# Converting float64 weights to fp32 on chip: signs and exponents by two parametric Relus on ScalarE, mantissas joined as integers, and the last products and the last store issued another way

## The chip, the cores and the metric

The kernel runs on one core of one Trainium2 chip. The metric is the device time of one execution in microseconds, as the median of several. A core has five engines with queues of their own: TensorE (PE, with its weight loads PEld), VectorE (DVE), ScalarE (ACT), GpSimd (POOL) and SyncE (SP), which here only issues DMAs. They wait for each other by semaphores; each takes its own instructions in the order in which the program gives them.

## The reference

Two blocks are computed, the second on the result of the first. The first is a recurrence over 768 steps for 4 batches and 8 heads, with a state of 40 x 40 for each; the second is a feed-forward block with the gate h * clip(h + 3, 0, 6) / 6.

```python
# r, k, v, w, a, b: (4, 8, 768, 40), float32
for t in range(S):
    y[:, :, t] = einsum('bhd,bhde->bhe', rt, state)
    Sa = einsum('bhde,bhe->bhd', state, at)
    state = state * wt[:, :, None, :] - einsum('bhd,bhe->bhde', Sa, bt) \
            + einsum('bhd,bhe->bhde', vt, kt)
x = y.transpose(0, 2, 1, 3).reshape(3072, 320)
h = x @ w_in                                  # 320 x 2048
out = (h * clip(h + 3.0, 0.0, 6.0) / 6.0) @ w_out     # 2048 x 320
```

The two weight matrices come as float64 (a division by a float64 root made them so), everything else as float32. [...] the kernel reads the weights as pairs of 32-bit words and makes fp32 of them itself.

## The kernel before

**Units and groups.** The sequence is cut into blocks of 64 steps; a unit is one block of two batches, with all 8 heads. There are 24 units, in groups of four. For a unit the recurrence becomes matrix products: running products of w (a scan on VectorE, L484) and their reciprocals (L495, L510), scaled a, b and k (at L513, bt L521, kt L603), scores (L458, masked by L467), the inverse of a triangular matrix, and from these the update of the state (sn, L865 and L874), the output y (L889, then yg, L898 to L904) and a transposed copy of it, xt, moved by DMAs from SBUF to SBUF (L918, L923).

**The inversion.** It is done for a whole group at once (invert, from L643). F is transposed in blocks of 32 (fb, L648), masked on POOL (L651), then 30 steps follow, each a product (prod, L660) and an addition (x, L666), each dependent on the one before; two transposes (tb L669, tt L674) end it. third_block (L696 to L729) completes the 64 x 64 inverse tinv.

**The feed-forward block.** For each unit there are two jobs of half the hidden features each. expand makes 24 products (L974; the trace records each fp32 product as two), of which 8 use the third part of the 320 features, win2 (these are the "short" ones); ScalarE and VectorE make the gate of them (gt, L989 and L990) in two halves; contract makes 8 products with wout (L1015), ScalarE copies the sum out (L1033) and two DMAs store it (L1038). While spread is on, a job's short products are not issued by expand but through narrow, by contract of the job before, after its sixth product (LATEST), or by the recurrence.

**The weights.** load_weights is a generator. There are 20 pieces of 128 x 512 weights, 512 KB of raw data each. A piece's raw words lie in one of eight homes, places whose own use comes later (tinv, parts of win and wout, the inversion's tiles), with low words and high words alternating. Its loads are issued on SyncE (L277), and a home is only loaded again when the conversion that frees it is in the program (the list free). Piece 15 needs piece 8 done, 16 needs 9, 17 needs 13, 18 needs 14, 19 needs 15.

Before the change the conversion of a piece is: the exponent field, shifted down, by VectorE (L299); ScalarE subtracts 896, times 2^23, with a Relu (L301); VectorE puts the sign bit on (L320); VectorE makes 2^23 plus the high mantissa bits as a float (L325), ScalarE scales that (L328); VectorE adds the low word times 2^-52 (L307) and multiplies by the power of two (L312). L307 and L312 of a piece come after L299 of the next one, so the pieces overlap by one.

**What sets the order of the work.** The schedule is manual: the order of the Python calls is the order of each engine's instructions, and generators are advanced to mix them. In the first group, by_twos runs the preparation of four units two by two (aside runs one step of the inversion). The weights' generator is advanced by one yield: by run, when a weight (its argument fill) is given; by aside, for each step, with the weight MIXED; in the loop after it (L1133 to L1142), at every third step of the inversion; then while phase says that a conversion is in a certain state; and from the list PLAN on, which orders the four first units' own work (U, UT, sn, H, y, move), 1.5 or 3 times for each entry, with the rest of the weights after it. limit says how many loads may have been issued so far. In the same loop tinv is cleared on POOL when two pieces are converted. The feed-forward jobs start when half the pieces (for the first half of units 0 and 1) or all of them are converted and the unit's xt is there; from then on pieces() mixes the feed-forward products with the recurrence to the end, and the last lines (while jobs or next(stream)) issue what is left.

Of the kernel before, what the change touches and what calls it, by code (L numbers as in the profile page):

```python
# [16 lines left out]
P = 128  # L17
BL = 64
HB = BL // 2
L = 32  # L20
SLOT = 64


def _ap(ap, extra, dims):
# [5 lines left out]
def kernel(  # L30
# [42 lines left out]
    nc = tc.nc  # L73
# [34 lines left out]
    def ps_pair(*dims):  # L108
# [19 lines left out]
        out=ident[:], in_=ones, pattern=[[1, P]],  # L128
# [4 lines left out]
        out=ones[:, 0:BL], in_=ones[:, 0:BL], pattern=[[1, BL]],  # L133
# [3 lines left out]
        out=ones[BL:P, 0:BL], in_=ones[BL:P, BL:P], pattern=[[1, BL]],  # L137
# [6 lines left out]
    nc.vector.memset(three[:], 3.0)  # L144
    warm = const.tile([P, 1], F32, name="warm")
    nc.scalar.activation(out=warm[:], in_=three[:], func=AF.Relu)
    low = const.tile([P, 1], F32, name="low")
    nc.vector.memset(low[:], -896.0 * 2 ** 23)


    AHEAD = NU + 1
# [33 lines left out]
    for i in range(3):  # L185
        t = const.tile([P, H, BL], F32, name=f"score{i}")
# [36 lines left out]
    converted = [0]  # L223
    phase = [0]
# [30 lines left out]
    def load_weights():  # L255

        todo, homes = weight_pieces(), raw_homes()
        loaded, done, issued = deque(), [], [0]
        upcoming = []

        def load():
            if issued[0] == min(PIECES, limit[0]):
                return False
            if not upcoming:
                upcoming.append(next(homes))
            raw, before = upcoming[0]  # L270
            if before is not None and before not in done:
                return False
            upcoming.clear()
            issued[0] += 1
            out, loads = next(todo)
            for to, src in loads(raw):
                nc.sync.dma_start(out=to, in_=src)  # L277
# [12 lines left out]
        for n in range(PIECES + 1):  # L290
            now = None
            if n < PIECES:
                while load():
                    pass
                out, raw = loaded.popleft()
                hi = raw[:, :, :, 1]
                x = parts[n % 2]
                now = out, raw, x
                nc.vector.tensor_scalar(x, hi, 20, 0x7FF, ALU.logical_shift_right,  # L299
                                        ALU.bitwise_and)  # L300
                nc.scalar.activation(out=x, in_=x, func=AF.Relu, bias=low[:], scale=2.0 ** 23)  # L301
                phase[0] = 1
                yield
            if before:
                out, raw, y = before
                m, yf = raw[:, :, :, 1].bitcast(F32), y.bitcast(F32)
                nc.vector.scalar_tensor_tensor(m, raw[:, :, :, 0], 2.0 ** -52, m, ALU.mult, ALU.add)  # L307
                phase[0] = 2
                yield
                if len(out.shape) == 4:  # L310
                    m, yf = (z.rearrange("p n (j c) -> p n j c", c=out.shape[3]) for z in (m, yf))
                nc.vector.tensor_tensor(out=out, in0=m, in1=yf, op=ALU.mult)  # L312
                converted[0] += 1
                done.append(n - 1)
                while load():
                    pass
                phase[0] = 3
                yield
            if now:
                nc.vector.scalar_tensor_tensor(x, hi, 0x80000000, x, ALU.bitwise_and,  # L320
                                               ALU.bitwise_or)
                phase[0] = 4
                yield

                nc.vector.tensor_scalar(hi, hi, 0xFFFFF, 0x4B000000, ALU.bitwise_and,  # L325
                                        ALU.bitwise_or)
                m = hi.bitcast(F32)
                nc.scalar.activation(out=m, in_=m, func=AF.Copy, bias=-7.0, scale=2.0 ** -20)  # L328
                phase[0] = 5
                yield  # L330
            before = now

    def weight_pieces():

# [47 lines left out]
    NK = NG * NU  # L382
# [65 lines left out]
    def half(i, n=SLOT):  # L448
        return slice(SLOT * i, SLOT * i + n)
# [489 lines left out]
    narrow, spread, LATEST = [], [False], 2  # L939
# [67 lines left out]
    def contract(i, r, gts):  # L1007
        split = i < SPLIT
        if r == 0 or split:
            op = bank("o", [P, DM], 1)  # L1010
        else:
            op = sums.pop(i)
        for c in range(2):
            for n in range(NQ):
                nc.tensor.matmul(out=op[:], lhsT=gts[c][:, n, :],  # L1015
                                 rhs=wout[:, c * HJ + r * NQ + n, :],
                                 start=((split or r == 0) and c == 0 and n == 0),
                                 stop=((split or r == 1) and c == 1 and n == NQ - 1))
                if n % 2 and (c == 0 or n < NQ - 1):
                    yield True  # L1020
        if r == 0:
            sums[i] = op
            if split:
                part = ffn.tile([P, 3 * P], F32, name="part", tag="xt", bufs=6)[:, 0:DM]
                nc.scalar.activation(out=part, in_=op[:], func=AF.Copy, scale=1.0 / 6.0)
                sums[i] = part
        else:
            ob = ffn.tile([P, DM], F32, name="ob", bufs=OB)
            if split:
                nc.vector.scalar_tensor_tensor(out=ob[:], in0=op[:], scalar=1.0 / 6.0,  # L1030
                                               in1=sums.pop(i), op0=ALU.mult, op1=ALU.add)
            else:
                nc.scalar.activation(out=ob[:], in_=op[:], func=AF.Copy, scale=1.0 / 6.0)  # L1033
            del ready[i]
            g, p = names[i]
            for q in range(2):
                row = (2 * p + q) * T + g * BL
                nc.sync.dma_start(out=out[row:row + BL, :], in_=ob[half(q)])  # L1038
        yield True


# [45 lines left out]

    STAGES = 9

    RFETCH, EARLY, MIXED = 8, 5, 1 / 3  # L1090
    TWOS = 14

    def by_twos(first, steps, mixed, rate, fill={}):


        chains = [by_stages(first + i, prepared(first + i)) for i in range(NU)]
        for t in range(TWOS):

# [14 lines left out]
    for name in "WABK":  # L1113
        for i, engine in enumerate((nc.sync, nc.scalar if name == "W" else nc.sync)):
            fetch(name, i, engine)
    for t, _ in enumerate(by_twos(0, 4, MIXED, 0, {5: 1, 6: 1, 10: 1})):
        if t == 0:
            next(weights)
        limit[0] = {7: 4, 10: 12}.get(t, limit[0])
        while t == 7 and refill[0]():  # L1120
            pass
        if t == RFETCH:
            fetch("R", 0)
# [8 lines left out]
    n, cleared = 0, []  # L1132
    while not third:  # L1133
        aside(1)
        if not third:
            n += 1
            if n % 3 == 1:
                next(weights, None)
            if converted[0] == 2 and not cleared:
                cleared.append(nc.gpsimd.memset(tinv[:], 0.0))  # L1140
            if n % EARLY == 0 and early:
                run(early.popleft())  # L1142
    assert not early and cleared
# [161 lines left out]
    m = 0  # L1305
# [60 lines left out]
```

## Time and profile before

| | |
|---|---|
| median of three runs | 831.4 us (829.04 to 831.72) |
| the profiled execution | 831.98 us; its span, first to last instruction, 830.2 us |
| mean granted TensorE clock | 0.938 |
| busy: TensorE / weight loads | 746.4 us (90%) / 632.0 us (76%) |
| busy: VectorE / ScalarE / POOL | 547.4 us (66%) / 321.7 us (39%) / 156.1 us (19%) |
| HBM read / written | 34.08 MB / 3.93 MB |

The page gives the busy time of each engine, then the span in 40 slices of 20.8 us: a digit is the busy share of an engine in tenths, and the row PEclk gives the TensorE clock that was granted, in tenths of full speed. The chain that ended last is found by going back from the last instruction, each time to what released it. A line "L301 ACT ACTIVATE parts<-parts,low" is an instruction of line 301 on ScalarE that writes the tile parts and reads parts and low. In a timeline the first column is the start, the second the duration, both in us; what stands in brackets is the time for which the engine stood idle before, and what released it. SPq are DMAs as they are issued by SyncE. A table by stretches gives for each engine the busy time and the number of instructions, and then the clock, the share of the DMA engines and GB/s.

The stretches of the start in the trace before:

| us from the start | TensorE busy | VectorE busy | ScalarE busy | clock |
|---|---|---|---|---|
| 20 to 40 | 16.08 | 19.14 | 7.55 | 0.70 |
| 40 to 60 | 5.99 | 18.23 | 5.64 | 0.55 |
| 60 to 80 | 4.57 | 19.25 | 4.60 | 0.50 |
| 80 to 100 | 16.10 | 12.69 | 14.77 | 0.58 |
| 100 to 120 | 16.19 | 17.29 | 10.05 | 0.74 |
| 120 to 140 | 12.77 | 16.00 | 9.98 | 0.77 |
| 140 to 160 | 16.76 | 17.95 | 5.71 | 0.89 |
| 160 to 180 | 19.23 | 17.64 | 6.51 | 1.00 |

### The profile page before, as it was taken

Reading aid. Unit: us, or ns where it says so; the run is one execution under the profiler, and the core shown is the slowest. Engines: PE = TensorE matmul, PEld = TensorE weight load, DVE = VectorE, ACT = ScalarE, POOL = GpSimd, SP = SyncE. Lnnn points to the kernel's source line nnn. Section 1 sums busy time; section 2 is a strip of 40 time slices with the busy share of each in tenths; the row PEclk is TensorE's granted clock in tenths of the full one; section 3 lists DMA queues with packets and bytes.
Section 4 is the critical chain, followed back from the end, with each engine's and each line's share of the span. In section 5 each row is a group of like instructions: output and inputs, shape, how many; then the busy total and the mean of one; then the engine's idle time right before and its main releaser. Section 6 shows DMA issues by size and latency. Waiting matters only on the chain.

```text
span 830.2 us, 35843 instructions
## 1 busy us (share of the span) xinstructions
PE 746.4 (90%) x15832; PEld 632.0 (76%) x15832; DVE 547.4 (66%) x1108; ACT 321.7 (39%) x864; POOL 156.1 (19%) x305
## 2 busy tenths in 40 slices
PE   4732877898999999999999999999999999999997
PEld 3622766686887878788888888878888888888875
DVE  7999697988964769844589654799556685232201
ACT  1323744232344533454433635334553334322211
POOL 3231301122112230321220222112212102000000
PEclk7755587999999999999999999999999999999999
DMA  7573344331133230322331332232232101100000
GB/s 141 85 187 85 91 113 100 70 62 25 21 59 65 52 66 19 59 46 48 56 51 28 60 62 44 42 58 36 45 60 48 22 20 29 29 20 16 15 18 16
DMA packets 174218, 45.05 MB, mean 54 GB/s; under 512 B 157424, under 2 KB 172784, under 8 KB 174064
## 3 DMA queue, kind: packets, MB, share of 16 engines
q1 hardware_dynamic: 171920, 42.44, 26.8%
q8 instruction: 125, 2.05, 1.0%
q10 hardware_dynamic: 2144, 0.33, 0.2%
q14 instruction: 29, 0.24, 0.1%
HBM read 34.08 MB, written 3.93 MB: 46 GB/s over the span
## 4 chain that ended last, share of the span: by engine, by line
PE 70%; DVE 12%; issue 9%; ACT 3%; POOL 2%; DMA 1%; SPq 0%; POOLq 0%; DVEq 0%; ACTq 0%
PE h L974 24%; PE o L1015 22%; PE any L458 4%; PE any L889 3%; PE any L420 2%; PE any L430 2%; PE any L865 2%; DVE prod L660 2%; DVE x L666 2%; PE any L770 1%; PE any L809 1%; DVE parts L320 1%; PE any L830 1%; PE any L846 1%; PE any L696 1%
## 5 line engine op out<-in xcount | busy, mean ns | idle before, releaser
L974 PE MATMUL h<-xt,win 128*128 128x128 f32 (+1 forms) x2304 | 252.8, 284 | 7.0 <-DVE gt L990 7.0
L974 PEld LDWEIGHTS h<-xt,win 128*128 128x128 f32 (+1 forms) x2304 | 232.5, 193 | 25.8 <-issue 8.8
L1015 PE MATMUL o<-wout,gt 128*128 128x320 f32 x768 | 232.8, 445 | 0.2 <-DVE gt L990 0.2
L1015 PEld LDWEIGHTS o<-wout,gt 128*128 128x128 f32 x768 | 139.0, 191 | 51.2 <-issue 1.4
L989 ACT ACTIVATE gt<-h,three 128x512 f32<-128x512 f32 x96 | 62.1, 686 | 104.6 <-PE h L974 104.4
L990 DVE SCALAR_TENSOR_TENSOR gt<-gt,h 128x512 f32<-128x512 f32 x96 | 61.5, 677 | 61.2 <-ACT gt L989 61.2
L660 DVE TENSOR_TENSOR prod<-x 128x30 f32<-128x30 f32 (+9 forms) x180 | 62.8, 349 | 13.5 <-POOL x L651 8.1
L904 POOL TENSOR_TENSOR yg<-ys,gam 128x512 f32<-128x512 f32 x22 | 39.1, 1778 | 167.9 <-DVE ys L902 121.9
L874 DVE TENSOR_TENSOR state<-any,state 40x160 f32<-40x160 f32 (+1 forms) x88 | 27.9, 321 | 62.7 <-PE any L865 36.3
L666 DVE TENSOR_TENSOR x<-x,prod 128x30 f32<-128x30 f32 (+9 forms) x180 | 65.2, 362 | 5.4
L590 POOL TENSOR_TENSOR KBt<-K,rgt 128x320 f32<-128x320 f32 x24 | 21.1, 880 | 248.1 <-ACT rgt L580 217.3
L467 DVE COPY_PREDICATED score<-mask,any 128x256 f32<-128x256 int32 x143 | 53.4, 436 | 4.0 <-PE any L458 3.6
L495 DVE RECIPROCAL gam<-prods 128x256 f32<-128x256 f32 x24 | 41.5, 1741 | 13.5 <-POOL yg L904 13.2
L510 DVE RECIPROCAL rgam<-prods 128x256 f32<-128x256 f32 x24 | 41.8, 1741 | 0.0
L484 DVE TENSOR_TENSOR_SCAN prods<-wm,start 128x528 f32<-128x528 f32 x24 | 30.1, 1254 | 16.6 <-ACT wm L481 14.9
L623 ACT ACTIVATE EV<-any 64x160 f32<-64x160 f32 x92 | 24.8, 295 | 39.8 <-PE any L617 30.3
L902 DVE TENSOR_TENSOR ys<-any,ys 128x256 f32<-128x256 f32 x44 | 16.6, 418 | 34.1 <-PE any L617 18.3
L749 ACT ACTIVATE RT<-any 128x256 f32<-128x256 f32 (+1 forms) x44 | 15.5, 400 | 49.6 <-PE any L430 49.5
L889 PE MATMUL any<-score,KBt 64*64 64x64 f32 x1536 | 31.2, 232 | 2.4 <-DVE score L467 1.6
L889 PEld LDWEIGHTS any<-score,KBt 64*64 64x64 f32 x1536 | 27.5, 144 | 5.3 <-DVE score L467 1.7
L729 ACT ACTIVATE tinv<-any 32x256 f32<-32x256 f32 (+1 forms) x56 | 19.3, 344 | 28.9 <-PE any L719 28.1
L775 DVE TENSOR_TENSOR RR<-any,EV 128x160 f32<-128x160 f32 x44 | 12.2, 318 | 25.6 <-PE any L458 25.4
(193 smaller groups left out, 1077.4 us busy)
## 6 DMA issues: line engine op xcount, KB each, us to landing
B<-in_b_dram SPq DMA_DIRECT2D x48, 80.0 KB
K<-in_k_dram SPq DMA_DIRECT2D x48, 80.0 KB
V<-in_v_dram SPq DMA_DIRECT2D x96, 40.0 KB
out_dram<-ob SPq DMA_DIRECT2D x48, 80.0 KB
R<-in_r_dram SPq DMA_DIRECT2D x92, 40.0 KB
W<-in_w_dram SPq DMA_DIRECT2D x40, 80.0 KB
A<-in_a_dram SPq DMA_DIRECT2D x40, 80.0 KB
xt<-yg SPq DMA_DIRECT2D x72, 40.0 KB
```

Of the source, the lines that this page charges most:

```text
L458: nc.tensor.matmul(out=o[i][half(q), n, :], lhsT=lhs[half(i, D), n ^ (2 * q * swap), half(q)], rhs=rhs[half(i, D), n, half(q)], start=True ...
L467: nc.vector.copy_predicated(out=x[:, 4 * i:4 * i + 4, :], mask=mask4, data=o[i])
L495: nc.vector.reciprocal(gv[:, :, 0:HB], o["prods"][:, :, 0, 1:HB + 1][:, :, ::-1])
L510: nc.vector.reciprocal(rv[:, :, HB:BL], o["prods"][:, :, 1, 1:HB + 1])
L660: nc.vector.tensor_tensor(out=pv, in0=_ap(x[:], (i + 1) * L + i, [[L, n], [0, i]]), in1=_ap(x[:], i * L, [[0, n], [1, i]]), op=ALU.mult,)
L666: nc.vector.tensor_tensor(out=rest, in0=rest, in1=pv, op=ALU.add)
L889: nc.tensor.matmul(out=y[q][half(s), pr, :], lhsT=o[name][half(q), h * D:h * D + SLOT], rhs=m[name][half(q), 4 * rs + 2 * s + j, :], start ...
L904: nc.gpsimd.tensor_tensor(out=yg[:], in0=m["ys"][:].rearrange("p r q t -> p r (q t)"), in1=o["G"][:], op=ALU.mult)
L974: nc.tensor.matmul(out=hp[c][:, i, :], lhsT=lhsT, rhs=rhs, start=(begun[c] == 0), stop=(begun[c] == 3 * NQ - 1))
L989: nc.scalar.activation(out=gt[:], in_=hp[c][:], func=AF.Relu, bias=three[:], scale=1.0)
L990: nc.vector.scalar_tensor_tensor(out=gt[:], in0=gt[:], scalar=6.0, in1=hp[c][:], op0=ALU.min, op1=ALU.mult)
L1015: nc.tensor.matmul(out=op[:], lhsT=gts[c][:, n, :], rhs=wout[:, c * HJ + r * NQ + n, :], start=((split or r == 0) and c == 0 and n == 0), ...
```

## The change

**The conversion.** VectorE now keeps the twelve upper bits of the high word, sign and exponent, as they are (one mask). ScalarE reads them as a signed integer and applies a Prelu to -x / 2^20 + 916 - 1792, with slope 2^-40 for negative arguments, writing a float; a second Prelu takes -2^63 times that with a bias of -1792 * 2^23, the same slope, and writes an integer. For a positive weight the first lands on the small slope and the second undoes the scale, for a negative one the other way round; the integer that comes out is the bit pattern of a power of two with the weight's sign (the exponent is lowered by a constant, since the mantissa is now 2^20 to 2^21). VectorE makes the mantissa's high part an integer with its leading one (a mask and an or), adds the low word times 2^-32 to it as numbers, and multiplies. So a piece has four VectorE operations where it had five, and two ScalarE operations as before, but these now follow one another directly. The addition no longer waits for ScalarE.

**Its place.** A piece's product now comes right after the next piece's mask, and the two mantissa operations follow it. The generator yields four times for a piece, not five. fill is dropped in the first group, MIXED goes from 1/3 to 0.27, and the loop advances the weights at every fourth step instead of every third; the clearing of tinv comes when at least two pieces are converted; after the loop only a started piece's product is brought in. In the built program no piece operation now comes before the inversion's first product (six did), 16 come up to its second last transpose (27 did), and 64 after it (73). Nothing else moves on TensorE, apart from the end. On SyncE the loads of B and K for unit 4 come after the loads of pieces 4 to 7, and one load of R before that of piece 8. On POOL the clearing of tinv comes one copy later.

**The end.** After the last block of the recurrence spread is set to off, so the last three jobs' short products are issued in expand, before the eight wout products of the job before them and not between the sixth and the seventh. The second store of the last unit is issued by ScalarE.

```diff
-    low = const.tile([P, 1], F32, name="low")
-    nc.vector.memset(low[:], -896.0 * 2 ** 23)
+    low = const.tile([P, 2], F32, name="low")
+    for i, x in enumerate((EXP - 1792.0, -1792.0 * 2 ** 23)):
+        nc.vector.memset(low[:, i:i + 1], x)
...
-                nc.vector.tensor_scalar(x, hi, 20, 0x7FF, ALU.logical_shift_right,
-                                        ALU.bitwise_and)
-                nc.scalar.activation(out=x, in_=x, func=AF.Relu, bias=low[:], scale=2.0 ** 23)
+                nc.vector.tensor_scalar(x, hi, 0xFFF00000, None, ALU.bitwise_and)
+                nc.scalar.activation(out=x.bitcast(F32), in_=x.bitcast(I32), func=AF.Prelu, bias=low[:, 0:1],
+                                     scale=-2.0 ** -20, alpha=2.0 ** -40)
+                nc.scalar.activation(out=x.bitcast(I32), in_=x.bitcast(F32), func=AF.Prelu, bias=low[:, 1:2],
+                                     scale=-2.0 ** 63, alpha=2.0 ** -40)
                 phase[0] = 1
                 yield
             if before:
-                out, raw, y = before
-                m, yf = raw[:, :, :, 1].bitcast(F32), y.bitcast(F32)
-                nc.vector.scalar_tensor_tensor(m, raw[:, :, :, 0], 2.0 ** -52, m, ALU.mult, ALU.add)
-                phase[0] = 2
-                yield
...
+                to, m, yf = before
...
+                nc.vector.tensor_tensor(out=to, in0=m, in1=yf, op=ALU.mult)
                 converted[0] += 1
                 done.append(n - 1)
...
             if now:
-                nc.vector.scalar_tensor_tensor(x, hi, 0x80000000, x, ALU.bitwise_and,
-                                               ALU.bitwise_or)
+                nc.vector.tensor_scalar(hi, hi, 0xFFFFF, 0x100000, ALU.bitwise_and, ALU.bitwise_or)
+                phase[0] = 3
+                yield
+                m = hi.bitcast(F32)
+                nc.vector.scalar_tensor_tensor(m, raw[:, :, :, 0], 2.0 ** -32, hi, ALU.mult, ALU.add)
+                before = out, m, x.bitcast(F32)
                 phase[0] = 4
                 yield
-                nc.vector.tensor_scalar(hi, hi, 0xFFFFF, 0x4B000000, ALU.bitwise_and,
-                                        ALU.bitwise_or)
-                m = hi.bitcast(F32)
-                nc.scalar.activation(out=m, in_=m, func=AF.Copy, bias=-7.0, scale=2.0 ** -20)
-                phase[0] = 5
-                yield
...
-                nc.sync.dma_start(out=out[row:row + BL, :], in_=ob[half(q)])
+                queue = nc.scalar if q and i == NK - 1 else nc.sync
+                queue.dma_start(out=out[row:row + BL, :], in_=ob[half(q)])
...
-    RFETCH, EARLY, MIXED = 8, 5, 1 / 3
+    RFETCH, EARLY, MIXED = 8, 5, 0.27
...
-    for t, _ in enumerate(by_twos(0, 4, MIXED, 0, {5: 1, 6: 1, 10: 1})):
+    for t, _ in enumerate(by_twos(0, 4, MIXED, 0)):
...
-            if n % 3 == 1:
+            if n % 4 == 1:
                 next(weights, None)
-            if converted[0] == 2 and not cleared:
+            if converted[0] >= 2 and not cleared:
...
-    while phase[0] in (1, 2, 3):
+    while phase[0] == 1:
         next(weights)
...
+    spread[0] = False
     while jobs or next(stream):
         next(stream)
```

More of the change, by code (lines that the diff above doesn't have):

```diff
@@ L21 @@
 SLOT = 64
+EXP = 916
 def _ap(ap, extra, dims):
@@ L304, in load_weights @@
             if before:
-                out, raw, y = before
-                m, yf = raw[:, :, :, 1].bitcast(F32), y.bitcast(F32)
-                nc.vector.scalar_tensor_tensor(m, raw[:, :, :, 0], 2.0 ** -52, m, ALU.mult, ALU.add)
-                phase[0] = 2
-                yield
-                if len(out.shape) == 4:
-                    m, yf = (z.rearrange("p n (j c) -> p n j c", c=out.shape[3]) for z in (m, yf))
-                nc.vector.tensor_tensor(out=out, in0=m, in1=yf, op=ALU.mult)
+                to, m, yf = before
+                if len(to.shape) == 4:
+                    m, yf = (z.rearrange("p n (j c) -> p n j c", c=to.shape[3]) for z in (m, yf))
+                nc.vector.tensor_tensor(out=to, in0=m, in1=yf, op=ALU.mult)
                 converted[0] += 1
@@ L316, in load_weights @@
                     pass
+                phase[0] = 2
+                yield
+            before = None
+            if now:
+                nc.vector.tensor_scalar(hi, hi, 0xFFFFF, 0x100000, ALU.bitwise_and, ALU.bitwise_or)
                 phase[0] = 3
                 yield
-            if now:
-                nc.vector.scalar_tensor_tensor(x, hi, 0x80000000, x, ALU.bitwise_and,
-                                               ALU.bitwise_or)
+                m = hi.bitcast(F32)
+                nc.vector.scalar_tensor_tensor(m, raw[:, :, :, 0], 2.0 ** -32, hi, ALU.mult, ALU.add)
+                before = out, m, x.bitcast(F32)
                 phase[0] = 4
                 yield
-                nc.vector.tensor_scalar(hi, hi, 0xFFFFF, 0x4B000000, ALU.bitwise_and,
-                                        ALU.bitwise_or)
-                m = hi.bitcast(F32)
-                nc.scalar.activation(out=m, in_=m, func=AF.Copy, bias=-7.0, scale=2.0 ** -20)
-                phase[0] = 5
-                yield
-            before = now
     def weight_pieces():
```

## The prediction

> **What bounds the kernel now.** I read the 40 slices of the page first, then the chain that ended last in order of time, then the timelines of VectorE, SyncE and the end. In the page's slices:
>
> ```profile
> PE   4732877898999999999999999999999999999997
> DVE  7999697988964769844589654799556685232201
> PEclk7755587999999999999999999999999999999999
> ```
>
> From about 170 us (the ninth slice) TensorE is nearly full and at full clock; nothing that VectorE saves there is worth time. The first 160 us (some 8 slices) are different: VectorE is busy, TensorE is not, and its granted clock is half. The weights are unpacked exactly there (line L299 first at 23.3 us, L312 last at 156.5 us). The chain of waits in this stretch runs through the unpacking:
>
> ```profile
> 120.00 0.69 ACT raw_fb L328
> 120.71 0.70 DVE raw_fb L307
> 121.44 0.69 DVE win L312
> 122.13 0.47 DVE state L874 x2
> 122.60 0.61 DVE parts L320
> ...
> 126.58 0.61 DVE gt L990
> 127.24 1.98 PE h L974 x8
> ```
>
> Each piece costs VectorE five operations and sends VectorE to ScalarE and back (L325 to L328 to L307, with VectorE idle about 0.4 us); the feed-forward's first matmuls wait behind it. Earlier, 43.6 to 77.7 us, the chain is the triangular inversion (prod and x), one dependent VectorE operation after the other, with pieces slipped in:
>
> ```profile
> 58.27 0.40 DVE L660 TENSOR_TENSOR prod<-x 128x234 f32<-128x234 f32 x1
> 58.59 0.68 DVE L312 TENSOR_TENSOR win<-raw,parts 128x512 f32<-128x512 f32 x1
> 59.19 0.40 DVE L666 TENSOR_TENSOR x<-x,prod 128x234 f32<-128x234 f32 x1
> 59.62 0.41 DVE L660 TENSOR_TENSOR prod<-x 128x238 f32<-128x238 f32 x1
> ```
>
> Without a guest, x to prod is 0.43 us (59.19 to 59.62); with one, prod to x is 0.92 (58.27 to 59.19). So a 0.68 us guest costs 0.49 us here, and a 0.42 us guest 0.22 (61.87 to 62.53 less 0.44), the rest hiding the dependency. Last, SyncE's queue, whose order the change keeps from here on:
>
> ```profile
> 96.70 3.31 SPq L403 DMA_DIRECT2D R<-in_r_dram  x4
> ...
> 116.35 2.46 SPq L923 DMA_DIRECT2D xt<-yg  x4
> 118.92 1.43 SPq L277 DMA_DIRECT2D raw<-in_moe_w_out_dram  x1
> ```
>
> From 96.70 to 123.4 us it issues without a pause, about 0.74 us a DMA (32 DMAs to 120.35). The load at 118.92 is piece 16 (counted from 0).
>
> **What the Trainium skill says.** "VectorE: DVE Perf Modes", walkthrough of the 8-slice pipeline, mode 2x_2P: fp32 work with one source can run at two elements a cycle, with two sources at one. The trace agrees: 0.42 us for tensor_scalar (L299, L325), 0.68 to 0.69 for two sources (L307, L312, L320). "ScalarE: Activation LUTs", what happens when an exp ACTIVATE runs: one element per cycle whatever the function. No run here shows a Prelu; I price it by the Relu with the same bias operand (L301, 0.72 us). The same page, what ACT_TABLE_LOAD costs: a function outside the loaded set costs about 2.7 us. The trace has one load (1.28 us, at 0.80), and the changed program also has one, so nothing is added. "TensorE: Matmul & The Clock Gate", part 1: the clock halves after an idle window of about 3.4 us and comes back after a busy one; the trace shows 0.50 at 152 to 154 us after TensorE's idle stretch near 149 to 150.
>
> **The change, part by part.**
>
> *VectorE's work.* Per piece, L299 0.42, L320 0.685, L325 0.42, L307 0.685, L312 0.69 become mask 0.42, mask 0.42, mantissa add 0.685, product 0.69. One 0.685 us operation goes: 20 x 0.685 = 13.7 us, and the ping-pong through L328 with it. That is not the gain; it has to be followed stage by stage.
>
> *20 to 43 us.* Four piece operations stood ahead of the reciprocals (23.32 to 27.20) and two (L307, L312) ahead of the transpose fb; none do now, as the early filling is gone. VectorE alone would be 3.9 us earlier. But bt and kt of units 2 and 3 need B and K, whose loads SyncE issues to 33.13 us, and K lands some 2.5 us later (as R does: issue ends 59.70, TensorE resumes 62.46). Their start hangs on KBt (POOL, L590), which gains 2 to 3 us since ScalarE does rgt before any piece, yet W's issue ahead of them ends only at 25.96 instead of B's start at 26.96. So they gain 0.9 to 1.8 us, and the order bt, kt, F then allows about 2.7 us to the start of the inversion. Taken: 2.7 (bounds 1 and 4.5).
>
> *The inversion, 43.6 to 79.7 us.* Before, 20 guests: 12 x 0.49 + 8 x 0.22 = 7.6 us. By the new order 16: 7 x 0.49 + 9 x 0.22 = 5.4 us. Gain 2.2. Together 4.9 us at the end of the transposes.
>
> *80 to 127 us.* Unpacking moves later: 64 piece operations follow the inversion, 73 before. In the packed run a piece took about 3.2 us with its wait (L299 at 116.65 to L299 at 119.88); now 0.34 + 0.60 + 0.46 + 0.60 = 2.0 us from the starts of such rows. VectorE could be some 3 us early at piece 16 beyond the 4.9. But piece 16 has to be there. Its DMA stands behind R and two sets of xt moves in SyncE's queue; the memory burst that follows its issue is seen at:
>
> ```profile
> 122.00:123.00 1.00, 1.00 (x11) 0.97 (x9) 1.00 (x4) 0.00 (x0) 0.00 (x0) 1.00 1.06 378
> 123.00:124.00 1.00, 1.00 (x18) 0.91 (x16) 0.96 (x4) 0.31 (x1) 0.00 (x0) 1.00 1.10 214
> ```
>
> (the last column is GB/s), so it lands near 123.5. Before, nobody noticed, as VectorE took it up only at 128.0. In the new order gt's operations stand behind piece 16 on both engines: mask at 123.5, then on ScalarE two Prelus of 0.72 each, the second waiting for the first, S 0.57 and gt 0.7, so gt on VectorE starts about 126.65 against 126.50: 0.15 us lost. Queued behind the waiting mask are a score mask, piece 15's product and gt; the matmul of 127.24 waits for gt. Also, the two Prelus of piece 6 stand before zs (91.46 before): sn ends about 0.5 us earlier because L301 no longer precedes U, but state, mantissa add (0.60), mask, and 1.45 us of Prelus push zs to 91.9: 0.45 us lost, which moves R's load and so the whole queue. Net of this stage: 0.6 us given back.
>
> *127 to 158 us.* Pieces 17 to 19 land in time (issues from 123.44 on, bursts at 126 and 128). U of unit 3 waits for piece 18's Prelus, where it waited for L328 at 134.60: about even, 0.35 later. From there the end of the unpacking is out of the way: the state addition (147.85, behind scans and three pieces' operations) and the score mask (149.98) come 3 to 5 us earlier, TensorE's waits of 0.87 and 1.56 us before L889 go, and y ends 2.1 us earlier instead of 0.15 later: a gain of 2.25. With no hole there, the eight L1015 matmuls that took 4.07 us at half clock may take 2.35: I take 1 of the possible 1.7.
>
> *After 158 us* TensorE's order is the same and it is full, so what is gained stays.
>
> *The end.*
>
> ```profile
> 826.62 1.11 SPq L1038 DMA_DIRECT2D out_dram<-ob  x2
> ```
>
> The last two stores are issued one after the other; the second now goes out from ScalarE, idle then: 0.55 us. With spread off, the last short products are issued within their expansion, so TensorE no longer waits 0.22 us for gt, three times (802.19, 811.84, 821.50): 0.66. Together 1.2 us.
>
> *At nothing.* One memset more for the constants: VectorE idles 3.4 us before its first scan. On SyncE the B and K loads of unit 4 (four DMAs, 46.17 to 49.7) move behind nine weight loads, which so leave 3 us earlier; unit 4's B and K are used after 157 us, a cover of 90 us. On POOL the clearing of tinv (1.80 us) moves behind one 0.3 us copy and has 20 us before the first write to tinv at 79.8.
>
> *Sum.* 4.9 - 0.6 + 2.25 + 1.0 + 1.2 = 8.75 us from the profiled execution's 831.98 (span 830.2): 823.2. The median of the runs, 831.4, is 0.6 below it; I forecast 822.8.
>
> **Rivals.**
>
> 1. *The loads don't bind.* If piece 16 lands before VectorE gets to it (its queue moves up with R's earlier consumer, or the bursts are shorter), the 3 us and the 0.6 come back, and the second stage's 13.7 us is nearly all kept: 13.7 + 1.2 = 14.9, time 816.5. For: TensorE idles 18 us between 80 and 160. Against: the unbroken queue.
> 2. *Only the inversion and the end gain.* TensorE or DMA in 127 to 158 keeps its pace and the clock isn't granted; the start gains 1 us only: 1.0 + 2.2 - 0.6 + 1.2 = 3.8, time 827.6. For: R, B and K loads are already nearly late at 34 us.
> 3. *Slower: the loads chain up.* Places 15 to 19 of raw data are freed by products 8, 9, 13, 14, 15; if each of the four last loads comes late, VectorE stalls at each, with scores, gt and state queued behind it. At 3.4 us from issue to landing only piece 16 waits. Each 1 us beyond that costs about 4 us; the 8.75 us are gone at 5.6 us, and at 6 us it is 833. Against: every 512 KB burst here was over in 3 to 4 us.
> 4. *It doesn't do what it says:* Prelu at double price, 20 x 2 x 0.72 = 29 us more on ScalarE, half of it before zs, tinv, U, UT: about level, 831. Against: the skill's flat price.
>
> **How the numbers follow.** The forecast 60%, rival 1 16%, rival 2 14%, rival 3 5%, rival 4 5%. The range takes the first three without the far half of rival 1's side: 815 to 829. About 0.3% (2.5 us) is what a measurement of this kernel can tell from no change. Faster 0.91, same 0.04, slower 0.05.
>
> **What would show it.** In the changed profile: about 0.72 us for each Prelu and a pair of 1.45; the second transpose of the inversion ending near 76.5 instead of 81.5; VectorE waiting 1 to 3 us for the DMA of raw before piece 16's mask near 119; gt near 122; TensorE without holes before its first L889 after L1015; no 0.22 us waits and one store from each queue at the end. Wrong if Prelu is not priced like Relu, if no wait on that load shows, or if a DMA wait after 160 us takes the gain back.

## The result, and the profile after

| | before | changed |
|---|---|---|
| median of 6 runs each | 831.91 us (829.04 to 834.17) | 824.33 us (821.78 to 827.35) |
| profiled execution / its span | 831.98 / 830.2 us | 823.69 / 822.0 us |
| busy: VectorE / ScalarE / TensorE | 547.4 / 321.7 / 746.4 us | 532.8 / 324.6 / 742.9 us |

The ratio is 0.9909, with a 95% interval of 0.9891 to 0.9928: 7.6 us less, where 822.8 us were forecast. The slices of the page after:

```profile
PE   4724867998999999999999999999999999999998
DVE  6889587978855679834699654799556685232210
PEclk7755687999999999999999999999999999999999
```

As before, TensorE is full from the ninth slice on, and what changed lies ahead of it. The two Prelus are in the list of groups (ScalarE, line, shapes, count, busy time, mean ns):

```profile
L304 ACT ACTIVATE parts<-parts,low 128x512 int32<-128x512 f32 x20 | 14.4, 722 | 0.7
L302 ACT ACTIVATE parts<-parts,low 128x512 f32<-128x512 int32 x20 | 14.4, 722 | 37.1 <-DVE parts L301 36.9
```

Each takes 0.72 us, as the Relu did. But the answer that matters is where the same work stands in time in the two traces (new line numbers are about three lower than the old ones):

| start of | before | changed | difference | as the prediction's steps sum up |
|---|---|---|---|---|
| first product of the inversion | 43.64 | 42.38 | -1.3 | -2.7 |
| its first transpose (tb) | 77.75 | 74.28 | -3.5 | -4.9 |
| first load of R after it, SyncE | 96.70 | 93.35 | -3.4 | |
| load of piece 16, SyncE | 118.92 | 116.87 | -2.1 | |
| gt, first job | 126.50 | 124.51 | -2.0 | -4.3 |
| eight wout products of the first job | 151.31 | 145.77 | -5.5 | |
| next eight wout products | 169.16 | 161.78 | -7.4 | -7.55 |
| last copy to ob | 826.16 | 818.18 | -8.0 | -8.75 (end) |

The lines behind it, from VectorE's timeline of the changed kernel (start, duration; in brackets the idle time before and what ended it):

```profile
121.48 0.43 DVE L301 TENSOR_SCALAR parts<-raw 128x512 uint32<-128x512 uint32 x1 [3.08 <-DMA raw<-in_moe_w_out_dram]
...
124.51 1.29 DVE L987 SCALAR_TENSOR_TENSOR gt<-gt,h 128x512 f32<-128x512 f32 x2 [0.28 <-ACT gt L986]
```

and from TensorE's:

```profile
125.26 2.07 PE L971 MATMUL h<-xt,win 128*128 128x128 f32 x8 [5.59 <-DVE gt L987]
...
133.82 0.86 PE L455 MATMUL any<-RT,VT 40*64 40x64 f32 x30 [2.79 <-ACT U L811]
...
145.77 2.42 PE L1012 MATMUL o<-wout,gt 128*128 128x320 f32 x8
```

The last of these stood like this in TensorE's timeline before the change:

```profile
150.47 0.92 PE L889 MATMUL any<-score,KBt 64*64 64x64 f32 x32 [1.56 <-DVE score L467]
151.31 4.07 PE L1015 MATMUL o<-wout,gt 128*128 128x320 f32 x8
```

VectorE waits 3.08 us for piece 16's raw words, gt stands behind it, and TensorE idles 5.59 us, more than the 2.99 us before. Then the picture turns: the eight L1012 products have no wait ahead of them, and take 2.42 us where they took 4.07 at half clock (0.50 at 152 to 154 us). At the end no wait of 0.22 us is left, and the last two stores are issued at 818.65 us, one from each queue.

### The profile page after: what moved, and what is told of

Its sections match the earlier page's. It is cut to its first block, busy times and chain, and to the rows that moved or that the text cites. A ratio compares the mean times of both kernels' runs of the same rounds, so it can differ in the third digit from the quotient of the medians.

```text
span 822.0 us, 35812 instructions
## 1 busy us (share of the span) xinstructions
PE 742.9 (90%) x15832; PEld 632.0 (77%) x15832; DVE 532.8 (65%) x1089; ACT 324.6 (39%) x864; POOL 155.0 (19%) x305
## 4 chain that ended last, share of the span: by engine, by line
PE 63%; issue 9%; DVE 4%; POOL 2%; DMA 1%; ACT 1%; SPq 0%; POOLq 0%; DVEq 0%; ACTq 0%
PE h L971 23%; PE o L1012 20%; PE any L455 3%; PE any L886 2%; PE any L427 2%; PE any L417 2%; PE any L862 2%; PE any L806 1%; PE any L767 1%; PE any L843 1%; PE any L827 1%; PE any L790 1%; PE any L614 1%; POOL KBt L587 1%; POOL yg L901 1%
## 5 line engine op out<-in xcount | busy, mean ns | idle before, releaser
L1012 PE MATMUL o<-wout,gt 128*128 128x320 f32 x768 | 230.0, 442 | 0.0
L1012 PEld LDWEIGHTS o<-wout,gt 128*128 128x128 f32 x768 | 138.1, 190 | 50.3
L302 ACT ACTIVATE parts<-parts,low 128x512 f32<-128x512 int32 x20 | 14.4, 722 | 37.1 <-DVE parts L301 36.9
```

Source lines behind the costliest of these rows:

```text
L1012: nc.tensor.matmul(out=op[:], lhsT=gts[c][:, n, :], rhs=wout[:, c * HJ + r * NQ + n, :], start=((split or r == 0) and c == 0 and n == 0), ...
```

## The experiments

Twelve kernels, each timed beside the kernel before. Ratios are to that kernel, with 95% intervals. In no kernel is a part of the computation left out.

### The end alone

The kernel before with the edits at the end (spread set to off, last store on ScalarE).

> The kernel before with the two edits at the end alone (spread off after the recurrence, second store of the last unit from ScalarE). My theory: no 0.22 us waits before the last wout products and one 0.55 us issue less, 1.2 us off: 830.7 us, ratio 0.9985. Rival: the end is bound by the store's own landing and by TensorE's weight loads, so nothing is gained: 831.9. Everything before 780 us should be unchanged in both.

Measured: 830.81 us, ratio 0.998 (0.9969 to 0.9991): 1.7 us by the ratio, 1.3 by the medians (832.15 before). The end gains, about what was priced or a little more. For the last five contractions and the three expansions between them the changed kernel needs 36.28 us (781.82 to 818.10), where 37.75 were needed (788.33 to 826.08): 1.47, of which the three waits are 0.66. A job's period goes from 9.65 to 9.17 us; what the remaining 0.26 a job is, the trace doesn't say (TensorE turns between the two kinds of product four times a job before, twice now). From the last copy to the end of the span there are 3.82 us where there were 4.04: the second queue is worth about 0.2, not 0.55.

### The old placement with the new conversion, and the new placement with the old conversion

```diff
-    RFETCH, EARLY, MIXED = 8, 5, 0.27
+    RFETCH, EARLY, MIXED = 8, 5, 1 / 3
-    for t, _ in enumerate(by_twos(0, 4, MIXED, 0)):
+    for t, _ in enumerate(by_twos(0, 4, MIXED, 0, {5: 1, 6: 1, 10: 1})):
-            if n % 4 == 1:
+            if n % 3 == 1:
```

> The changed kernel with the old placement of the pieces (weight 1/3, the early filling, every third step). Theory: the placement makes the gain up to the end of the inversion (3.5 us in the changed kernel's trace), so here the inversion starts and ends within 1 us of before (tb near 77 us); 53 piece operations instead of 73 then follow it, so VectorE reaches gt early, but piece 16 still waits for its load, and the total comes to 826 to 829 us, ratio about 0.995. Rival A: the conversion alone makes everything, 824. Rival B: only the placement and the end count, 830.7.

> The kernel before with the new placement alone (conversion and end as before): no piece operation ahead of the inversion, 16 up to its second last transpose, 84 after it (before: 73). Theory: the inversion ends 3 to 3.5 us early as in the changed kernel, but the 11 operations more after it, about 0.6 us each with their waits, give back more than that: 833 to 836 us, ratio 1.001 to 1.005. Rival: the pieces after the inversion are hidden behind loads and TensorE, then the 3.5 us stay: 828.4.

Old placement, new conversion: 824.45 us, 0.9916 (0.9899 to 0.9933). New placement, old conversion, old end: 841.8 us, 1.013 (1.01 to 1.0161). Both differ from what I expected, the second by far.

With the old placement the inversion ends where it did before (tb at 77.77), as expected, but VectorE then runs out of loaded data. Its timeline:

```profile
126.02 0.43 DVE L301 TENSOR_SCALAR parts<-raw_fb 128x512 uint32<-128x512 uint32 x1 [8.45 <-DMA raw_fb<-in_moe_w_out_dram]
...
134.12 1.28 DVE L987 SCALAR_TENSOR_TENSOR gt<-gt,h 128x512 f32<-128x512 f32 x2 [2.07 <-ACT gt L986]
```

8.45 us of idle VectorE, gt nearly 8 us later than before the change; and yet the next eight wout products start at 164.82, 4.3 us earlier than before: by 137 us no unpacking is left to stand in the way, where before the change it went on to 157 us.

The other half explains why the two edits belong together. With the new placement and five operations a piece, everything up to 161 us is 4.2 us early (U of unit 3 at 131.01, bt at 161.25 against 165.46), but the last piece is multiplied at 171.40 us, where it was at 156.52 before and at 141.49 in the changed kernel. Between 160 and 200 us TensorE is busy for 30.04 us where it was busy for 36.03, at a mean clock of 0.87 where it was 0.96. ScalarE's and TensorE's timelines show the first cause:

```profile
169.99 0.66 ACT L328 ACTIVATE raw<-raw 128x512 f32<-128x512 f32 x1 [2.85 <-DVE raw L325]
...
170.97 1.13 PE L458 MATMUL any<-at,kt 40*64 40x64 f32 x30 [3.78 <-ACT F L541]
```

The operations of the last two pieces fill VectorE from 163.63 to 172.0 us, in the middle of the next group's preparation, and ScalarE copies that group's F (L541, 170.55) only behind L328 of the last piece. TensorE waits 3.78 us for F, 1.99 for gt at 181.69, and 5.43 before 201.69 (where the profile names nothing that it waited for), against 3.20 at the same place before; after the first and the last of these its clock is at 0.50. One and the same product of the recurrence (L846), 5.1 us early at 136.4 us, is 6.9 us late at 242.2 and 9.9 us late at 295.1. At the end nothing more is lost: from the first contraction after the recurrence on, both kernels need 37.75 us (799.64 to 837.39 and 788.33 to 826.08). So it was not 0.6 us for each added operation, as I had expected, but unpacking that lasts into the next group's preparation. What share comes from these waits and what share from the built order, in which feed-forward jobs start when all pieces are converted, was not tried apart.

### The changed kernel beside its old placement

Since the two were only 0.1 us apart in different sets of runs, both ran again side by side.

> The changed kernel itself, as the measure for the three beside it: 824.3 us, ratio 0.991.

> The changed kernel with the old placement once more, now beside the changed kernel. In the traces it was 2.1 us behind at the end (span 824.1 against 822.0) and 3 us at the first full contraction, while the medians of the two were 0.1 us apart. Theory: the placement is worth the trace's difference, so 1 to 3 us more than the changed kernel. Rival: it is worth nothing, within 0.7 us.

Measured: 825.08 us, 0.9912 (0.9895 to 0.9929), and 826.2 us, 0.9932 (0.9914 to 0.995). Over both sets (11 and 12 runs) the means are 824.7 and 825.7 us, 1.0 us apart with an uncertainty of 1.4. The placement is worth something between nothing and 2 us; the theory's 1 to 3 and the rival's 0 are both still possible. The traces of this pair are also closer than those of the first: the second eight wout products start at 163.02 and 163.52 us, where they started at 161.78 and 164.82. In this second profile of the changed kernel piece 16's mask waits 1.39 us for its load, not 3.08.

### One more VectorE operation for each piece

```diff
                 nc.vector.tensor_scalar(hi, hi, 0xFFFFF, 0x100000, ALU.bitwise_and, ALU.bitwise_or)
+                nc.vector.scalar_tensor_tensor(hi, hi, 0x100000, hi, ALU.bitwise_or, ALU.bitwise_or)
```

> The changed kernel with one more two-source VectorE operation for each piece, between the mantissa mask and the mantissa add: it sets bits that are set already, so nothing else changes. 20 x 0.69 = 13.7 us of VectorE come back, as in the kernel before, but without its way through ScalarE. Theory: what a VectorE operation costs depends on where it stands; about 4 in the inversion at 0.49 us are 2 us, those ahead of piece 16's wait for its load are hidden by it, and the four last pieces cost up to 2 us more: 826 to 829 us (ratio 0.993 to 0.996). Rival A: VectorE's time counts in full, 838. Rival B: it was the way through ScalarE alone that cost, and VectorE's work is hidden: 824.5.

Measured: 831.25 us, 0.9996 (0.9982 to 1.0011). One operation of 0.69 us takes nearly the whole gain back, about 7 us; my 2 to 5 were too low, and neither rival holds. The trace says why. In the inversion (VectorE; line 322 is the added one):

```profile
53.98 0.42 DVE L321 TENSOR_SCALAR tinv<-tinv 128x512 uint32<-128x512 uint32 x1
54.44 0.69 DVE L322 SCALAR_TENSOR_TENSOR tinv<-tinv 128x512 uint32<-128x512 uint32 x1
55.05 0.38 DVE L658 TENSOR_TENSOR prod<-x 128x220 f32<-128x220 f32 x1
```

From the mask to the next prod there are 1.07 us where the changed kernel has 0.33 (53.80 to 54.13): 0.74 us for the operation, not 0.49. The cheap price holds for a single guest that hides a dependency; the second in a row pays its full step, and here also its wait for the mask. Four such make 3.0, and the inversion (first prod to tb) is 3.1 us longer: 35.03 against 31.90. Up to piece 16's mask there are 12 more, 8.8 us at the same price, of which 2.9 arrive: the 3.08 us wait for the load is gone (the mask starts at 126.80 without one), and by the difference about 2.8 us of other waits with it. So the wait hides some of VectorE's work, as expected, but not all of it: 12 operations were more than it could cover. Behind it the four last pieces cost 1.15. In sum 7.2 us, less 0.7 by which this execution started earlier: 6.5 at the second set of wout products (168.25 against 161.78).

### The loads issued by another queue

```diff
-                nc.sync.dma_start(out=to, in_=src)
+                (nc.scalar if issued[0] == 17 else nc.sync).dma_start(out=to, in_=src)
```

> The changed kernel with one load (piece 16's raw words) issued by ScalarE instead of SyncE, so that it does not stand behind R and the xt moves. Theory (the load binds because of its place in SyncE's queue): the wait of 3.08 us before piece 16's mask goes, gt comes 2.5 to 3 us earlier, TensorE's hole of 5.6 us before it shrinks to about 3 and the total falls by 2 to 3 us, to 821.5 to 822.5 (ratio to before 0.987 to 0.989); what is late next is piece 17's load. Rival A: the DMA engines are full with the xt moves, so that the load lands no earlier: 824.3. Rival B: piece 17's load takes over the whole wait: gain under 1 us.

Measured: 825.47 us, 0.9916 (0.9893 to 0.9939): no gain. VectorE's timeline shows the reason, rival B:

```profile
121.71 1.28 DVE L987 SCALAR_TENSOR_TENSOR gt<-gt,h 128x512 f32<-128x512 f32 x2 [0.28 <-ACT gt L986]
127.33 0.43 DVE L301 TENSOR_SCALAR parts<-raw_fb 128x512 uint32<-128x512 uint32 x1 [4.33 <-DMA raw_fb<-in_moe_w_out_dram]
```

Piece 16 no longer waits, gt is 2.8 us earlier and TensorE's hole shrinks to 2.31 us; but piece 17's load, in the same SyncE queue, now keeps VectorE 4.33 us, and ys is queued behind it (TensorE waits 3.80 us for it). Part of this comes from the edit itself. Among the waits of SyncE's queue between 95 and 125 us (in total, times, longest) stands one that the changed kernel does not have:

```profile
SPq L920 <- DMA raw<-in_moe_w_out_dram: 3.3, 1, 3.3
```

An xt move on SyncE stands still until, by the profile, the load that ScalarE issued at 105.91 us has landed, and everything behind it in the queue moves back: piece 17's load goes out at 123.14, where it went out at 120.36. So the place in the queue does bind, but this kernel does not show what a free load would be worth. The next kernel moves all four (issued[0] >= 17).

> The changed kernel with the last four pieces' loads issued by ScalarE, as soon as the products that free their places are done. With piece 16's load alone moved, piece 17's mask waited 4.33 us in its place and the total did not fall. Theory: the place in SyncE's queue is the limit for all four, so now no mask waits over 1 us, ys comes 4 us earlier than 128.6 us, U of unit 3 near 129, and the total is 3 to 5 us under that of the changed kernel: 819.5 to 821.5, ratio 0.985 to 0.987. Rival A: the xt moves keep the DMA engines full, the loads land at the same time wherever they are issued: 824.3. Rival B: another wait between 125 and 160 us (scans, scores, TensorE at half clock) takes it back: 823 to 824, with ys early and the first contraction not.

Measured: 824.14 us, 0.9907 (0.9887 to 0.9926): again no gain, though piece 17's mask now runs at 123.08 us without a wait. Rival B of that kernel. TensorE's timeline of it:

```profile
130.98 1.13 PE L455 MATMUL any<-RT,VT 40*64 40x64 f32 x30 [3.35 <-ACT U L811]
...
160.03 4.11 PE L1012 MATMUL o<-wout,gt 128*128 128x320 f32 x8
```

Three things took the place of the load. First, the edit again has a cost of its own. ScalarE now issues the loads in its own order of work, and runs nothing between the end of one Prelu at 116.42 and the issue of piece 18's load at 118.34; piece 16's Prelus come only then, although its mask ended at 117.27:

```profile
118.76 0.72 ACT L302 ACTIVATE parts<-parts,low 128x512 f32<-128x512 int32 x1 [2.33 <-DVE wout L312]
```

Two more loads are issued ahead of S, and gt on VectorE waits 2.28 us for ScalarE (121.88) where it waited 0.28. What the issue at 118.34 waited for is not shown; the product that the bracket names (117.85, 0.68 us) ended after it. The xt move on SyncE waits too, 4.3 us. Second, ScalarE brings U only after the Prelus of piece 18:

```profile
129.26 0.72 ACT L302 ACTIVATE parts<-parts,low 128x512 f32<-128x512 int32 x1 [4.25 <-DVE parts L301]
130.02 0.72 ACT L304 ACTIVATE parts<-parts,low 128x512 int32<-128x512 f32 x1
130.65 0.48 ACT L811 ACTIVATE U<-any 128x160 f32<-128x160 f32 x2
```

and piece 18's mask is itself late: it started at 127.74 and took 1.49 us instead of 0.42, as GpSimd's yg ran from 127.36 to 128.94. The Trainium skill, "SBUF — State Buffer", Who interferes with whom, states that a VectorE operation in a two-port mode and a GpSimd operation exclude each other, the later one waiting for the end of the earlier; the trace agrees, as the mask ends 0.3 us after yg. (In the changed kernel the same mask takes 1.49 us as well, so this is no difference between the two.) Third, in this execution the second eight wout products came at half clock, 4.11 us instead of 2.42. Of the 1.75 us by which they start earlier than in the changed kernel (160.03 against 161.78), 1.5 were there at fb already (37.29 against 38.83), where the programs don't differ. So 0.2 us are left for the four moved loads (1.4 against the second profile of the changed kernel, with 163.02 and 38.93).

The same edit with the old placement, where the wait for piece 17 was 8.45 us:

> The old placement of the conversion, with the loads of pieces 16 to 19 issued by ScalarE. With the loads on SyncE, VectorE waited 8.45 us for piece 17's load, with gt behind it at 134.12 us. Theory: that wait is what the old placement loses after the inversion; without it gt comes 5 to 7 us earlier (127 to 129), and the total is 2 to 4 us lower, 821 to 823 (ratio 0.987 to 0.989). Rival: the wait is followed by TensorE's own (half clock, U behind the Prelus), so that ys and the first contraction move by less than 1 us: 824.5.

Measured: 822.18 us, 0.9873 (0.9852 to 0.9894), beside 826.2 us for the old placement with all loads on SyncE: 4.0 us, as expected, and 2.9 under the changed kernel of the same set. VectorE's timeline and TensorE's:

```profile
128.38 1.28 DVE L987 SCALAR_TENSOR_TENSOR gt<-gt,h 128x512 f32<-128x512 f32 x2 [2.01 <-ACT gt L986]
```

```profile
160.17 2.42 PE L1012 MATMUL o<-wout,gt 128*128 128x320 f32 x8
```

Piece 17's mask has no wait (118.12), and gt comes 4.8 us earlier than in the run beside it (133.20). No Prelu pair stands between gt and U here, TensorE doesn't wait for U, and the second wout products start 1.6 us ahead of the changed kernel's, although the inversion ended 4.3 us later. Here the load was the limit; in the new placement it was one of several that end within a few us of each other, and moving it cost part of what it could give.

### The start

B and K of units 2 and 3 are issued behind W of unit 4; this W now comes after V. On its own, with the four loads moved, and with the four loads in the old placement:

```diff
-            fetch("W", following(i))
+            if following(i) != 4:
+                fetch("W", following(i))
...
+            if following(i) == 4:
+                fetch("W", 4)
             fetch("A", following(i))
```

> The changed kernel with the load of W for unit 4 (two DMAs) moved in SyncE's queue from ahead of B and K of units 2 and 3 to behind V. Theory: the start up to the inversion is bound by those loads (TensorE waited 1.84 and 2.06 us for B at 30.6 and 33.3 us), so B, K come 1 to 1.4 us earlier, and so do fb and the inversion's start (41.2 instead of 42.4); the total gains about 1, 823.3 (ratio 0.9897). Rival A: the places of B and K come free too late, so nothing moves: 824.3. Rival B: the inversion starts earlier, but piece 16 and 17 take it back by their loads: the first part early, contraction at 161.8 as before, 824.3.

> Both last edits on the changed kernel: loads of pieces 16 to 19 from ScalarE, and W of unit 4 later. Theory: as the loads no longer hold back what was gained earlier, the two gains add up: 818.5 to 820.5, ratio 0.984 to 0.9865. Rival: whatever takes back the first edit's gain takes back this one's too, 823 to 824.

> As the kernel before this one, with W of unit 4 loaded later as well: by the start's share alone about 1 us less, 820 to 822. With the new placement both edits together gave 822.0. Rival: no difference to it within 0.7 us.

Measured: 822.53 us, 0.9894 (0.9873 to 0.9915); 821.99 us, 0.9875 (0.9854 to 0.9896); 824.33 us, 0.9909 (0.9888 to 0.993). B's first issue does move, from 26.41 to 25.23 us. But the three do not agree: with the new placement 1.8 and 2.2 us less than without the edit, with the old one 2.2 more, each within the intervals' overlap. Programs that are the same up to fb start it anywhere from 37.29 to 39.17 us, more than the edit could give. Whether it is worth anything stays open. The lowest two are the changed kernel with both edits (0.9875) and the old placement with the four loads on ScalarE (0.9873), some 3 us under the changed kernel; as they are the lowest of twelve, and as W moved in the second gave 0.9909, the true difference may be smaller.

## Why the prediction was right, and where it was not

The time was right to 1.5 us, but of the six steps only the inversion came out at its size. The others were off by 0.5 to 2.2 us, some one way and some the other, so the closeness of the sum is in part luck.

- *20 to 43 us: 2.7 us predicted, 1.3 measured.* It was said that B and K limit the gain to 0.9 to 1.8 us and then 2.7 was taken, by the order bt, kt, F. The first figure was the right one: TensorE waited twice for B (1.84 us before 30.64, 2.06 before 33.33), and K's issue ended only 0.6 us earlier than before (32.53 against 33.13). The 2.7 also counted L307 and L312 ahead of fb as time won. With them gone VectorE waits there for F instead, whose last copy ends only 0.45 us earlier than before (38.80 against 39.25), so fb gains 1.0:

```profile
38.83 2.13 DVE L645 STREAM_TRANSPOSE fb<-F 128x1024 f32<-128x1024 f32 x1 [1.97 <-ACT F L538]
```

- *The inversion: 2.2 predicted, 2.2 measured* (34.11 to 31.90 us). But the price of a guest is not a constant: the added operation cost 0.74.
- *80 to 127 us: 0.6 given back predicted, 1.5 measured.* The mechanism is the one described: piece 16's load behind R and the xt moves, 3.08 us of wait (1.39 in the second profile), gt queued behind it, and with the load moved to ScalarE this wait is gone. The load itself took what this step had taken, 4.6 us from issue (116.87) to use (121.48), as from 118.92 to 123.5 in the forecast. The mis-sized term is the queue ahead of it: from R to the load it took 23.5 us, where the 22.2 of before were carried over.
- *127 to 158 us: 2.25 and 1.0 for the clock predicted, 5.4 measured* (from 2.0 to 7.4). The state addition comes 5.6 us earlier (142.24 against 147.85) and the score mask 7.3 (142.71 against 149.98), where 3 to 5 were forecast; the waits of 0.87 and 1.56 us are gone, and the clock gave all of the 1.7 us, not 1. How much it gives depends on the execution: in the kernel with the end alone the same products took 3.46 us, not 4.07. U lost 0.3 us on gt, as predicted (0.35): the gain is all behind it.
- *After 158 us: nothing lost predicted.* Between 316 and 350 us 1.2 us went (UT of the recurrence from 7.7 to 6.5 us ahead), about when the clock was at 0.50 (339 to 342); one execution doesn't tell whether that recurs.
- *The end: 1.2 predicted, 1.7 measured* in the trace, and 1.3 to 1.7 by the kernel with this alone: the waits' 0.66 were 1.47, the store's 0.55 were 0.2.

Rival 1 (the loads don't bind, 816.5) did not come true: the wait is there, and the kernels that take it away gain 0 to 3 us. But those kernels put waits of their own in its place (3.3 to 4.3 us in SyncE's queue, 2 us on ScalarE), so what the change would give with loads that come in time was not measured. Rival 2's time was missed because the stretch it gave up gained most. Rival 3 (the loads chain up) counted on 3.4 us for a load and 4 us of loss for each 1 us more. The load took 4.6, but piece 17 waited 0.86 us and pieces 18 and 19 not at all, so the rule was too steep for this order. In the old placement piece 17's load kept VectorE waiting 8.45 us, and even there the kernel was faster than before. Rival 4 fell with 0.72 us a Prelu.

What made the gain is settled in part. VectorE's work counts: one two-source operation more for each piece, though not the one that was removed nor in its place, and the gain is gone (0.9996). The end has 1.3 to 1.7 us. The placement alone, with the old conversion, costs about 10 us, and with the new one it gives 0 to 2. That the parts don't add is shown; how the remaining 4 to 6 us of the new conversion divide between fewer operations and the way through ScalarE that fell away was not tried apart.

## What to carry to other kernels

The price of an instruction is that of the place where it stands: the same 0.69 us cost 0.49 as a lone guest between dependent operations, 0.74 as a second one, and about 0.24 (2.9 us for 12) ahead of a wait for a load. Before taking a wait away, list what would be ready last without it, and what the remedy itself will make wait: moved loads held SyncE's queue for 3.3 to 4.3 us and ScalarE for 2. One moved load was worth nothing, and four were worth 4 us in one order of the work and nothing measurable in another. Work put off must also end before the next stage needs the engine: the placement alone looked 4 us better at 161 us and cost 10 in the end. A new placement and a shorter operation should be tried together and each alone, since the one may lose what it wins with the other.

## What the runs showed of the hardware that was not expected

- A second ScalarE operation on the tile that the first has just written starts 0.76 us after it (129.26 to 130.02) at 0.72 us each; one that doesn't depend on it starts after 0.63 (130.02 to 130.65). Between two Prelus the dependence costs 0.13 us, with int32 in and fp32 out and the other way round.
- A load issued by ScalarE can hold SyncE's queue: with piece 16's load moved, an xt move on SyncE waited 3.3 us, by the profile for that load, and 4.3 us with four loads moved; in the changed kernel, with all loads on SyncE, that move had no such wait.
- TensorE's clock fell to half after idle stretches much shorter than the 5.59 us hole: in the kernel with four moved loads the 1 us slices are at 1.00 up to 160, 0.65 at 160 to 161 and 0.50 at 161 to 163, after gaps of 1.01 and 1.04 us within the 6 us before. In the changed kernel the same products followed gaps of 1.01 and 0.72 us at full clock. Before the change the half clock at 152 to 154 us came after gaps of 0.87 and 1.56 us. All of these are shorter than the idle window of about 3.4 us that the prediction takes from the Trainium skill, "TensorE: Matmul & The Clock Gate", Part 1; what decides within such a stretch, these traces don't show. Full or half clock for these eight products alone moves an execution by 1.7 us.
